# Gated linear attention and a squared-ReLU layer on one core: decays without a head mask, other fillers on TensorE, other due times

## The chip, the cores and the metric

The kernel runs on one core of a Trainium2 chip. The core has five engines with queues of their own: TensorE (PE in the profile, its weight loads PEld), VectorE (DVE), ScalarE (ACT), GpSimd (POOL) and SyncE (SP, which here only issues DMAs). The metric is device time of one execution in microseconds; the median of five runs of the kernel before is 180.68 us (179.46 to 181.27).

## The reference

For each of 4 batches and 8 heads a state of 48 x 48 is carried over 768 tokens; then all heads together, 384 wide, go through two dense layers.

```python
for t in range(S):
    state = alpha[:, :, t, :, None] * state + einsum('bhd,bhe->bhde', k[:, :, t], v[:, :, t])
    y[:, :, t] = einsum('bhd,bhde->bhe', q[:, :, t], state)
x = y.transpose(0, 2, 1, 3).reshape(3072, 384)
h = x @ w_in                 # 384 -> 2048
out = maximum(h, 0) ** 2 @ w_out   # 2048 -> 384
```

Inputs and the output are float32.

## The kernel before

**Units.** The tokens of a batch are cut into three stretches of 256, which makes 12 units, numbered so that units 0 to 3 are the first stretches of the four batches, 4 to 7 the second, 8 to 11 the last. A partition holds two neighbouring tokens (j = 0 and 1).

**Front of a unit** (`front`). The alphas become logarithms (ACT), and a matmul with a triangle of ones (`LINC`, `LSTR`) makes their running sums; ACT turns these into factors `EK` (by which k is multiplied) and `EQ` (for q). In the same step, called `m1`, products with the two columns of ones `ONES2` (L543, L604, L636) give each channel's sum over the whole unit, and ACT's exponential of it is `ACM`, the decay of the state from one unit to the next. Two heads share a weight load here, so such a product gives a column for each of the two heads; the mask matmul before it (`HSEL` by `HCOL`, L540, L601 and L634) puts -1000 where the row belongs to one head and the column to the other, so that the exponential is zero there. k and q with their factors (`QKS`) are transposed, on TensorE for units 0 to 2 and by a DMA on SyncE from unit 3 on (`tr0`, `tr1`, L711).

**Attention** (`scores`, `state`, `output`). Scores of k against q in psX and psZ (L889), masked on DVE into `PM` (L900); k by v for the state (L760), added up as `SMD`, `TMP` and `SBD`; the output from scores, v and state (L781 and L792, for units 0 to 2 L821 and L828). From unit 3 on the state products are cut by head, so that only the block of a head with itself is read. In units 0 to 2, `SMD` is multiplied by a mask `OWN`. The output is copied to bfloat16 (L920 or L922) and transposed into `XT`, on TensorE (L935) or by a DMA on SyncE (L941, units 4 to 10).

**Dense layers** (`moe`). Eight blocks of two times three matmuls of 256 columns (L992) into two PSUM banks; ReLU on ACT or DVE (L1000, L1002), square on DVE, ACT or POOL; then two output tiles of 16 matmuls of 384 columns (L1028) in four quarters each, copied (L1035) and stored from SyncE (L1038).

**What sets the order.** `Program.add` notes each operation with what it reads and writes, a cost and a due time. `Program.schedule` then goes through time with these costs: whenever an engine is free it takes, of the operations whose inputs are there, the one with the lowest due time. Operations with two possible engines go where they would end first. TensorE has one more rule: matmuls come in modes (whole array, row or column tiles), and if the one with the lowest due time has another mode, one in the present mode goes first when it is due not more than `AFFINITY` later:

```python
same = [x for x in avail[e] if x.mode[0] == mode and x.prio <= o.prio + self.AFFINITY]
```

The result is a fixed order on each engine; on the chip an engine runs its queue in that order and waits for semaphores. DMAs are part of the queue that issues them. Due times are 13000 apart from unit to unit, except for the first units, where `FRONT`, `ATTN` and `DENSE` (L357 to L359) give the start for a unit's front, attention and dense part. The last quarter of a unit's dense part, for example, is due at `DENSE` + 12787, its output at `ATTN` + 5600.

**Fillers.** `Program.fill` then goes along TensorE's order and puts matmuls of zeros (`ZERO`, into psO) in gaps, from the end of the clearing of `ZERO` on up to the first operation named `s2_` (the second dense product). It compares the planned start of the next operation with the time at hand.

**Loads.** SyncE issues the loads of units 0 and 1 at the start; GpSimd issues the v of unit 1, then w_in in two halves (as soon as unit 1's alpha has landed), unit 2's inputs and w_out in two halves.

Of the kernel before, what the change touches and what calls it, by code (L numbers as in the profile page):

```python
# [9 lines left out]
BF16 = mybir.dt.bfloat16  # L10
# [23 lines left out]
class Program:  # L34
# [177 lines left out]

    def fill(self, make, cost, until, gap, after, cold):


        new = []
        t = after.land + self.HOP
        cold += t
        for o in self.order["pe"]:
            while t < until and o.start - t > gap + (cost if t < cold else 0):  # L220
                f = Op({"pe": (make, cost)}, 0, "fill")
                f.idx = len(self.ops)
                f.eng, f.fn, f.cost = "pe", make, cost
                f.start, f.end = t, t + cost * (2 if t < cold else 1)
                f.deps = {after: True}
                self.ops.append(f)
                new.append(f)
                t = f.end
            new.append(o)
            t = max(t, o.end)  # L230
        for i, o in enumerate(new):
            o.pos = i
        self.order["pe"] = new
# [100 lines left out]
def bass_gla_recurrent__then__act_relu_squared_kernel(  # L334
# [10 lines left out]
    HD = H * D  # L345
# [10 lines left out]
    DMA_X = (4, 5, 6, 7, 8, 9, 10)  # L356
    FRONT = {0: 0, 1: 13357, 2: 25644, 3: 26390, 4: 37530, 5: 53567}  # L357
    ATTN = {1: 14618, 2: 26767, 3: 37301, 4: 52103}
    DENSE = {0: 19639, 1: 32250, 2: 48764, 3: 61983, 11: 158500}  # L359
    POOL_LOADS = {1: "v", 2: "akqv"}  # L360
# [39 lines left out]
    ONES2 = nc.alloc_sbuf_tensor("ones2", [128, 2], BF16)  # L400
    HSEL = nc.alloc_sbuf_tensor("hsel", [128, 128], BF16)
    HCOL = nc.alloc_sbuf_tensor("hcol", [128, H], BF16)
    OWN = nc.alloc_sbuf_tensor("own", [128, H], BF16)
# [21 lines left out]
    def fill(buf, val):  # L425
        return lambda e: e.memset(buf, val)  # L426
# [91 lines left out]
    def front_by_heads(g, p0):  # L518
# [7 lines left out]
        for x in range(2):  # L526
# [63 lines left out]
    def decays_by_token(g, p0, r, la):  # L590
# [5 lines left out]
        def m1(pe):  # L596
            pe.matmul(bank[:, 0, 0:HD], LINC[:], LAF[la][:, 0, :, 0:D], start=True, stop=False)
            pe.matmul(bank[:, 1, 0:HD], LINC[:], LAF[la][:, 0, :, 0:D], start=True, stop=False)
            pe.matmul(bank[:, 1, 0:HD], LINC[:], LAF[la][:, 1, :, 0:D], start=False, stop=True)
            pe.matmul(bank[:, 0, 0:HD], LSTR[:], LAF[la][:, 1, :, 0:D], start=False, stop=True)  # L600
            pe.matmul(bank[:, 0, HD:HD + H], HSEL[:], HCOL[:], start=True, stop=False, skip_group_check=True)  # L601
# [7 lines left out]
        add("pe", m1, pe_ns(4, HD) + pe_ns(9, 8), p0 + 300,  # L609
            reads=[("laf", la), ("linc",), ("lstr",), ("ones",), ("hsel",), ("hcol",)], writes=keys, name=f"m1{g}")  # L610
        add("act", lambda e: e.activation(EK[la][:], bank[:, 0:2, 0:HD], AF.Exp, scale=-1.0), act_ns(2 * HD), p0 + 500,
# [6 lines left out]
    def decays_by_pair(g, p0, r, la, last):  # L618
# [11 lines left out]
        def m1(incl):  # L630
            def run(pe):
                ins = pe.matmul(psW[:, 0:HD], (LINC if incl else LSTR)[:], LAB[la][:, :, 0:D])
                if incl and not last:
                    pe.matmul(psW[:, HD:HD + H], HSEL[:], HCOL[:], start=True, stop=False, skip_group_check=True)  # L634
                    for p in range(NPR):
                        ins = pe.matmul(psW[:, HD + 2 * p:HD + 2 * p + 2],  # L636
                                        LAB[la][:, 2 * p:2 * p + 2, :].rearrange("p h d -> p (h d)"), ONES2[:],
                                        start=False, stop=True, skip_group_check=True)
                return ins
            return run  # L640

        add("pe", m1(True), pe_ns(1, HD) + (0 if last else pe_ns(5, 8)), p0 + 300,
            reads=[("lab", la), ("linc",), ("ones",), ("hsel",), ("hcol",)], writes=[("ps", "W")], name=f"m1i{g}")
        add("act", lambda e: e.activation(EK[la][:, 1, :], psW[:, 0:HD], AF.Exp, scale=-1.0), act_ns(HD), p0 + 500,  # L644
# [413 lines left out]
    for st in ORDER:  # L1058
# [9 lines left out]
        else:  # L1068
            output(g, kind == "w")
            moe(g)  # L1070
    pr.schedule()
    pr.fill(lambda pe: pe.matmul(psO[:, 0:256], ZERO[:, 0:128], ZERO[:, 0:256], skip_group_check=True), 109,  # L1072
            min(o.start for o in pr.order["pe"] if o.name.startswith("s2_")), 250, zero, 4600)
    pr.place()
# [29 lines left out]
```

## Time and profile before

| | |
|---|---|
| median of five runs | 180.68 us (179.46 to 181.27) |
| the profiled execution | 179.96 us, of which the span of the trace is 178.1 us |
| PE | busy 170.2 us, 96%, 2287 matmuls |
| DVE | busy 120.9 us, 205 instructions |
| ACT | busy 119.8 us, 214 instructions |
| POOL | busy 15.9 us, 25 instructions |
| first dense block | starts at 19.09 us |
| fillers (L1072) | 72 of 256 columns, first at 1.25, last at 27.8 us |

How to read it: times in a trace count from the first instruction, so the execution is 1.9 us longer than the span. A line of a timeline has the start, the time to the end of the last of a group, the engine, the line of the kernel, the operation, what it writes and reads, and the count; matmuls overlap, so the distance between starts tells more than their durations. In a list of waits, the numbers are total time, how often, and the longest.

### The profile page before, as it was taken

What the parts mean: (1) busy time and instruction counts of PE and PEld (TensorE: products, weight loads), DVE (VectorE), ACT (ScalarE), POOL (GpSimd) and SP (SyncE); (2) the same over time, 40 slices, a digit from 0 to 9 for tenths busy, and PEclk for the clock granted to TensorE, in tenths of its full rate; (3) what the DMA queues carried; (4) which work ended last, traced back from release to release, by engine and by line L of the source; (5) the groups of instructions that cost most, each with busy time, mean ns of one, the idle gap of its engine ahead of it and who ended that gap; (6) DMA issues with size and microseconds to landing.
All of it is one profiled execution on the core that took longest, in us unless ns stands there. A gap on an engine that the chain in (4) does not pass through costs nothing.

```text
span 178.1 us, 5220 instructions
## 1 busy us (share of the span) xinstructions
PE 170.2 (96%) x2287; PEld 135.4 (76%) x2287; DVE 120.9 (68%) x205; ACT 119.8 (67%) x214; POOL 15.9 (9%) x25
## 2 busy tenths in 40 slices
PE   7899999998999899999999999998999999999994
PEld 5777788865778679778778777785778787698773
DVE  6478499888749789958689678589669646342130
ACT  5466498567888788679489379578578374475541
POOL 3160632020102002010000000000000000000000
PEclk9999999999999999999999999999999999999999
DMA  4999999999989896899898798799999690110112
GB/s 114 267 314 191 232 305 214 229 293 263 224 185 218 212 234 154 227 239 147 219 252 180 190 246 185 189 242 190 242 185 220 156 198 19 44 48 0 44 48 88
DMA packets 74616, 33.18 MB, mean 186 GB/s; under 512 B 69889, under 2 KB 73089, under 8 KB 74593
## 3 DMA queue, kind: packets, MB, share of 16 engines
q1 hardware_dynamic: 72944, 27.73, 69.5%
q0 software_dynamic: 1648, 5.11, 12.9%
q8 instruction: 18, 0.29, 0.6%
q14 instruction: 6, 0.04, 0.1%
HBM read 25.17 MB, written 4.72 MB: 168 GB/s over the span
## 4 chain that ended last, share of the span: by engine, by line
PE 61%; DMA 19%; ACT 8%; DVE 6%; SPq 4%; issue 2%; DVEq 0%
PE psWH L992 28%; PE psO L1028 21%; DMA raw<-in_v_dram 7%; DMA win<-in_moe_w_in_dram 4%; ACT rr L1000 3%; DMA raw<-in_alpha_dram 3%; SPq L514 3%; DMA raw<-in_q_dram 3%; DMA xt<-xbf 2%; DVE pm L900 2%; PE psX L792 2%; PE psZ L760 2%; PE psX L962 1%; PE psX L889 1%; PE psX L781 1%
## 5 line engine op out<-in xcount | busy, mean ns | idle before, releaser
L992 PE MATMUL psWH<-xt,win 128*128 128x256 bf16 x576 | 73.7, 275 | 1.4 <-DMA xt<-xbf 0.9
L992 PEld LDWEIGHTS psWH<-xt,win 128*128 128x128 bf16 x576 | 65.0, 145 | 6.6 <-DMA xt<-xbf 1.3
L1028 PE MATMUL psO<-wout,gt 128*128 128x384 bf16 x368 | 69.1, 327 | 0.1
L1000 ACT ACTIVATE rr<-psWH 128x512 bf16<-128x512 f32 x82 | 47.8, 594 | 22.0 <-PE psWH L992 20.6
L1028 PEld LDWEIGHTS psO<-wout,gt 128*128 128x128 bf16 x368 | 35.0, 98 | 18.2 <-ACT osb L1035 0.3
L1010 DVE TENSOR_TENSOR gt<-rr 128x1024 bf16<-128x1024 bf16 (+1 forms) x39 | 22.8, 586 | 21.9 <-ACT rr L1000 21.8
L1014 ACT ACTIVATE gt<-rr 128x1024 bf16<-128x1024 bf16 (+1 forms) x21 | 18.4, 875 | 0.6
L900 DVE TENSOR_TENSOR pm<-psX,caus 128x1024 bf16<-128x1024 f32 x12 | 14.6, 1217 | 3.8 <-PE psZ L889 3.8
L900 DVE TENSOR_TENSOR pm<-psZ,caus 128x1024 bf16<-128x1024 f32 x12 | 14.6, 1217 | 2.7 <-PE psZ L889 2.7
L695 DVE TENSOR_TENSOR qks<-raw,eq 128x384 bf16<-128x384 f32 x18 | 9.3, 553 | 8.1 <-DMA raw<-in_q_dram 8.1
L1035 ACT ACTIVATE osb<-psO 128x384 f32<-128x384 f32 x19 | 9.3, 491 | 6.3 <-PE psO L1028 5.8
L691 ACT ACTIVATE vbf<-raw 128x768 bf16<-128x768 f32 x8 | 6.7, 842 | 9.0 <-DMA raw<-in_v_dram 9.0
L1072 PE MATMUL psO<-zero 128*128 128x256 bf16 x72 | 11.0, 304 | 1.3 <-DVE zero L426 1.3
L920 ACT ACTIVATE xbf<-psX 128x768 bf16<-128x768 f32 x11 | 8.8, 803 | 4.0 <-PE psX L781 2.0
L700 DVE TENSOR_TENSOR qks<-raw,ek 128x768 bf16<-128x768 f32 x11 | 11.3, 1024 | 0.0
L1002 DVE TENSOR_SCALAR rr<-psWH 128x512 bf16<-128x512 f32 x14 | 9.6, 684 | 0.9 <-PE psWH L992 0.6
L1072 PEld LDWEIGHTS psO<-zero 128*128 128x128 bf16 x72 | 7.2, 108 | 2.8 <-DVE zero L426 1.2
L666 ACT ACTIVATE la<-raw 128x384 f32<-128x384 f32 x8 | 4.2, 520 | 3.4 <-DMA raw<-in_alpha_dram 3.4
L623 DVE TENSOR_TENSOR prd<-raw 128x384 f32<-128x384 f32 x8 | 4.5, 557 | 2.8 <-DMA raw<-in_alpha_dram 2.8
L653 DVE TENSOR_TENSOR ek<-ek,raw 128x384 f32<-128x384 f32 x10 | 5.5, 553 | 0.8 <-ACT ek L644 0.7
L626 ACT ACTIVATE lab<-prd 128x384 bf16<-128x384 f32 x10 | 5.2, 521 | 1.1 <-DVE prd L623 0.8
L644 ACT ACTIVATE ek<-psWH 128x384 f32<-128x384 f32 x10 | 4.9, 493 | 1.4 <-PE psWH L636 1.4
(121 smaller groups left out, 164.9 us busy)
## 6 DMA issues: line engine op xcount, KB each, us to landing
out_dram<-osb SPq DMA_DIRECT2D x23, 192.0 KB, 2.4
raw<-in_k_dram SPq DMA_DIRECT2D x11, 384.0 KB, 4.8
raw<-in_q_dram SPq DMA_DIRECT2D x11, 384.0 KB, 4.3
raw<-in_v_dram SPq DMA_DIRECT2D x10, 384.0 KB, 5.6
raw<-in_alpha_dram SPq DMA_DIRECT2D x10, 384.0 KB, 4.0
win<-in_moe_w_in_dram POOLq DMA_DIRECT2D x2, 768.0 KB, 9.4
wout<-in_moe_w_out_dram POOLq DMA_DIRECT2D x2, 768.0 KB, 9.3
raw<-in_v_dram POOLq DMA_DIRECT2D x2, 384.0 KB, 5.9
```

What stands on the lines that cost most here:

```text
L695: add("dve", lambda e, j=j, dst=dst: e.tensor_tensor(dst, RAW[r][:, 2, :, j, :].rearrange("p (n x) d -> p n x d", x=2), EQ[la][:, j].rearr ...
L700: add("dve", lambda e, a=a, E=E: e.tensor_tensor(QKS[qs][:, a, :, :, 0:D], RAW[r][:, 1 + a].rearrange("p h j d -> p j h d"), E[la][:].rear ...
L900: add("dve", lambda e, hf=hf, psT=psT: e.tensor_tensor(PM[pm][:, hf].rearrange("p r n j t -> p (r n) (j t)"), psT[:, :, :].rearrange("p r ...
L920: add("act", lambda e: e.activation(XBF[x2][:], psX[:, :, 0:HD], AF.Copy), act_ns(2 * HD), p0 + 6100, reads=[("ps", "X", 0), ("ps", "X", 1 ...
L992: ins = pe.matmul(psH[hb][:, i * T:(i + 1) * T], WIN[:, kk, hidden(fj)], mov, start=(kk == 0), stop=(kk == KT - 1))
L1000: add("act", lambda e, hb=hb, rr=rr: e.activation(rr, psH[hb], AF.Relu), act_ns(512), pu + 600, reads=[("ps", "H", hb)], writes=[("rr", rb ...
L1002: alts={"dve": (lambda e, hb=hb, rr=rr: e.tensor_scalar(rr, psH[hb], 0.0, None, ALU.max), dve_ns(512))})
L1010: add("dve", lambda e, dst=dst, sq=sq: e.tensor_tensor(dst, sq, sq, ALU.mult), 148 + k * 267, pu + 1200, reads=[("rr", rb, h) for h in ran ...
L1014: "act": (lambda e, dst=dst, sq=sq: e.activation(dst, sq, AF.Square), act_ns(k * 512))})
L1028: ins = pe.matmul(psS, GT[gt][:, fj, j, :], WOUT[:, fj, :], start=(fj == 0), stop=(fj == FT - 1))
L1035: add("act", lambda e, ob=ob, psS=psS: e.activation(OSB[ob][:], psS, AF.Copy), act_ns(DM), ps_ + 700, reads=[keyS], writes=[("osb", ob)], ...
L1072: pr.fill(lambda pe: pe.matmul(psO[:, 0:256], ZERO[:, 0:128], ZERO[:, 0:256], skip_group_check=True), 109, min(o.start for o in pr.order[" ...
```

## The change

The buffers `HSEL` and `HCOL`, the memsets that fill them and the mask matmul in each `m1` are left out; the first product with ones then starts its accumulation itself where the mask did. `ACM` therefore holds the channel's decay in the columns of both heads, and the state's blocks between two heads are no longer zeroed. The fillers end at the first operation named `s1_` (the first dense product) and come in two widths, 512 columns (cost 216, in gaps over 420) before 256 (cost 109, over 250). Most of the due times of units 1 to 5 are other numbers.

```diff
-    def fill(self, make, cost, until, gap, after, cold):
+    def fill(self, make, sizes, until, after, cold):
...
-            while t < until and o.start - t > gap + (cost if t < cold else 0):
-                f = Op({"pe": (make, cost)}, 0, "fill")
+            while t < until:
+                slow = 2 if t < cold else 1
+                fits = [(n, c) for n, c, gap in sizes if o.start - t > gap + (slow - 1) * c]
+                if not fits:
+                    break
+                n, c = fits[0]
+                f = Op({"pe": (make(n), c)}, 0, "fill")
...
-                f.start, f.end = t, t + cost * (2 if t < cold else 1)
+                f.start, f.end = t, t + c * slow
...
-    FRONT = {0: 0, 1: 13357, 2: 25644, 3: 26390, 4: 37530, 5: 53567}
-    ATTN = {1: 14618, 2: 26767, 3: 37301, 4: 52103}
-    DENSE = {0: 19639, 1: 32250, 2: 48764, 3: 61983, 11: 158500}
+    FRONT = {0: 0, 1: 11855, 2: 27782, 3: 24892, 4: 39487, 5: 52627}
+    ATTN = {1: 13665, 2: 25972, 3: 40856, 4: 50288}
+    DENSE = {0: 21894, 1: 33515, 2: 47958, 3: 58770, 11: 158500}
...
-    for buf, key in ((HSEL, "hsel"), (HCOL, "hcol"), (OWN, "own")):
-        add("dve", fill(buf[:], 0.0), 100, -2e6, writes=[(key,)])
-    for part, key, val in ((HSEL[0:1, 64:128], "hsel", -1000.0), (HSEL[32:33, 0:64], "hsel", -1000.0),
-                           (HCOL[0:1, 0:H:2], "hcol", 1.0), (HCOL[32:33, 1:H:2], "hcol", 1.0),
-                           (OWN[0:64, 0:H:2], "own", 1.0), (OWN[64:128, 1:H:2], "own", 1.0)):
-        add("dve", fill(part, val), 100, -2e6, reads=[(key,)], writes=[(key,)])
+    add("dve", fill(OWN[:], 0.0), 100, -2e6, writes=[("own",)])
+    for part in (OWN[0:64, 0:H:2], OWN[64:128, 1:H:2]):
+        add("dve", fill(part, 1.0), 100, -2e6, reads=[("own",)], writes=[("own",)])
...
-                pe.matmul(bank[:, HD:HD + 4], HSEL[:], HCOL[:, 0:4], start=False, stop=False, skip_group_check=True)
...
-            add("pe", m1, pe_ns(4, N) + pe_ns(5, 8), px + 300,
-                reads=[("laf", la, x), ("linc",), ("lstr",), ("ones",), ("hsel",), ("hcol",)], writes=key,
+            add("pe", m1, pe_ns(4, N) + pe_ns(4, 8), px + 300,
+                reads=[("laf", la, x), ("linc",), ("lstr",), ("ones",)], writes=key,
...
-                    pe.matmul(psW[:, HD:HD + H], HSEL[:], HCOL[:], start=True, stop=False, skip_group_check=True)
                     for p in range(NPR):
                         ins = pe.matmul(psW[:, HD + 2 * p:HD + 2 * p + 2],
                                         LAB[la][:, 2 * p:2 * p + 2, :].rearrange("p h d -> p (h d)"), ONES2[:],
-                                        start=False, stop=True, skip_group_check=True)
+                                        start=(p == 0), stop=True, skip_group_check=True)
...
-    pr.fill(lambda pe: pe.matmul(psO[:, 0:256], ZERO[:, 0:128], ZERO[:, 0:256], skip_group_check=True), 109,
-            min(o.start for o in pr.order["pe"] if o.name.startswith("s2_")), 250, zero, 4600)
+    pr.fill(lambda n: lambda pe: pe.matmul(psO[:, 0:n], ZERO[:, 0:128], ZERO[:, 0:n], skip_group_check=True),
+            ((512, 216, 420), (256, 109, 250)), min(o.start for o in pr.order["pe"] if o.name.startswith("s1_")), zero, 4600)
```

More of the change, by code (lines that the diff above doesn't have):

```diff
@@ L219, in fill @@
         for o in self.order["pe"]:
-            while t < until and o.start - t > gap + (cost if t < cold else 0):
-                f = Op({"pe": (make, cost)}, 0, "fill")
+            while t < until:
[5 more added lines that the diff above has]
+                f = Op({"pe": (make(n), c)}, 0, "fill")
                 f.idx = len(self.ops)
-                f.eng, f.fn, f.cost = "pe", make, cost
-                f.start, f.end = t, t + cost * (2 if t < cold else 1)
+                f.eng, f.fn, f.cost = "pe", make(n), c
+                f.start, f.end = t, t + c * slow
                 f.deps = {after: True}
@@ L400, in bass_gla_recurrent__then__act_relu_squared_kernel @@
     ONES2 = nc.alloc_sbuf_tensor("ones2", [128, 2], BF16)
-    HSEL = nc.alloc_sbuf_tensor("hsel", [128, 128], BF16)
-    HCOL = nc.alloc_sbuf_tensor("hcol", [128, H], BF16)
     OWN = nc.alloc_sbuf_tensor("own", [128, H], BF16)
@@ L600, in m1 @@
             pe.matmul(bank[:, 0, 0:HD], LSTR[:], LAF[la][:, 1, :, 0:D], start=False, stop=True)
-            pe.matmul(bank[:, 0, HD:HD + H], HSEL[:], HCOL[:], start=True, stop=False, skip_group_check=True)
             for p in range(NPR):
@@ L605, in m1 @@
                                     LAF[la][:, j, 2 * p:2 * p + 2, :].rearrange("p h d -> p (h d)"), ONES2[:],
-                                    start=False, stop=True, skip_group_check=True)
+                                    start=(p == 0 and j == 0), stop=True, skip_group_check=True)
             return ins
-        add("pe", m1, pe_ns(4, HD) + pe_ns(9, 8), p0 + 300,
-            reads=[("laf", la), ("linc",), ("lstr",), ("ones",), ("hsel",), ("hcol",)], writes=keys, name=f"m1{g}")
+        add("pe", m1, pe_ns(4, HD) + pe_ns(8, 8), p0 + 300,
+            reads=[("laf", la), ("linc",), ("lstr",), ("ones",)], writes=keys, name=f"m1{g}")
         add("act", lambda e: e.activation(EK[la][:], bank[:, 0:2, 0:HD], AF.Exp, scale=-1.0), act_ns(2 * HD), p0 + 500,
@@ L637, in run @@
                                         LAB[la][:, 2 * p:2 * p + 2, :].rearrange("p h d -> p (h d)"), ONES2[:],
-                                        start=False, stop=True, skip_group_check=True)
+                                        start=(p == 0), stop=True, skip_group_check=True)
                 return ins
             return run
-        add("pe", m1(True), pe_ns(1, HD) + (0 if last else pe_ns(5, 8)), p0 + 300,
-            reads=[("lab", la), ("linc",), ("ones",), ("hsel",), ("hcol",)], writes=[("ps", "W")], name=f"m1i{g}")
+        add("pe", m1(True), pe_ns(1, HD) + (0 if last else pe_ns(4, 8)), p0 + 300,
+            reads=[("lab", la), ("linc",), ("ones",)], writes=[("ps", "W")], name=f"m1i{g}")
         add("act", lambda e: e.activation(EK[la][:, 1, :], psW[:, 0:HD], AF.Exp, scale=-1.0), act_ns(HD), p0 + 500,
```

## The prediction

> **What bounds the kernel now.** I read the page's first two parts, then the waits of TensorE, the chain that ended last, and the timelines of TensorE and SyncE around each edit.
>
> The page, share of each engine and the granted clock:
>
> ```profile
> PE 170.2 (96%) x2287; PEld 135.4 (76%) x2287; DVE 120.9 (68%) x205; ACT 119.8 (67%) x214; POOL 15.9 (9%) x25
> ...
> PEclk9999999999999999999999999999999999999999
> ```
>
> TensorE is busy 96% at a clock that never falls in any slice. The chain of waits of the first 21 us says what the start is:
>
> ```profile
> 3.03 2.54 SPq L514
> 5.57 0.04 issue
> 5.61 5.17 DMA raw<-in_alpha_dram
> 10.78 0.30 issue
> 11.08 7.87 DMA win<-in_moe_w_in_dram
> 18.95 0.14 issue
> 19.09 1.50 PE psWH L992 x12
> ```
>
> So the first dense block starts at 19.09 because the first half of w_in lands at 18.95; no TensorE work is on that path. From 19.09 to the last product TensorE is the path. All its idle time above the view's threshold, in the waits of TensorE after 18 us:
>
> ```profile
> PE psWH L992 <- DMA xt<-xbf: 0.9, 1, 0.9
> PE psX L821 <- DVE qks L700: 0.7, 1, 0.7
> PE psX L889 <- DVE la L668: 0.6, 1, 0.6
> PE psWH L992 <- DMA win<-in_moe_w_in_dram: 0.4, 1, 0.4
> ```
>
> 2.6 us in four places (124.8, 42.5, 60.0 and 19.1). Whatever is to move the time by over 1%, 1.8 us, must move the w_in landing, remove most of these, or make new waits.
>
> **The masks.** Nine mask matmuls go: two in unit 0 (L540), one in unit 1 (L601), one each in units 2 to 7 (L634). The weight load beside L634, in the timeline of unit 2:
>
> ```profile
> 27.25 0.33 PE L632 MATMUL psWH<-lab,linc 128*128 128x384 bf16 x1
> 27.25 0.10 PEld L634 LDWEIGHTS psWH<-hcol,hsel 128*128 128x128 bf16 x1
> 27.41 0.17 PE L634 MATMUL psWH<-hcol,hsel 128*128 128x8 bf16 x1
> 27.41 0.17 PEld L636 LDWEIGHTS psWH<-ones,lab 128*128 128x128 bf16 x4
> 27.44 0.24 PE L636 MATMUL psWH<-ones,lab 128*128 128x2 bf16 x4
> 27.54 0.60 PE L1072 MATMUL psO<-zero 128*128 128x256 bf16 x4
> ```
>
> The durations overlap, so starts are what counts: L632 holds the array from 27.25 to 27.41 with the mask there or not, the mask from 27.41 to 27.44, the four sums to 27.54. The mask's own load (27.25, 0.10) lies inside L632's time. One mask costs 0.03 us, six cost 0.18. The page's group for the chain agrees: L634 is 0.01 on it. Units 0 and 1 lie before 19.09: L540 takes 0.07 each (5.07 to 5.14, 5.84 to 5.91), L601 0.02. That is hidden: after the first of these, DVE waits for k ("DVE qks L567 <- DMA raw<-in_k_dram: 2.8" in the waits), and behind it stands w_in. If that cover went, it would be 0.16 more.
>
> [...]
>
> **The memsets.** Two whole buffers and four parts, six short memsets, go from DVE (2.07 to 2.58 us). DVE's next use that somebody waits for is at 6.97, when k has landed. Worth nothing; it would be 0.5 us if k came at once.
>
> **The fillers.** The page has 72 of 256 columns:
>
> ```profile
> L1072 PE MATMUL psO<-zero 128*128 128x256 bf16 x72 | 11.0, 304 | 1.3 <-DVE zero L426 1.3
> ```
>
> The timeline has 65 of them before 19.09, in gaps of 15, 6, 16, 2, 19, 1 and 6, then three at 23.00 and four at 27.54. After the change each gap before the first dense block is packed with 512-wide ones while more than 420 ns is left (636 while the clock is taken as cold), then with 256-wide ones while more than 250 is left (359 cold). Each old gap is its count times 109 ns (218 in the first, cold) and the rest that was too short for one more, so the new counts are about 7+1, 2+2, 7+2, 0+2, 9+2, 0+1 and 2+2: 27 wide and 12 narrow. A wide one is not in the trace; start to start a narrow one took 0.110 us warm and 0.213 cold, so a wide one takes at least one narrow, 0.110, and at most two, 0.22 and 0.43. I take two, since columns are what is streamed. In both versions a warm gap stays open for 0.14 to 0.25 us at its end, so the fillers end within 0.11 us of where they ended. The delay that they give to the matmul behind them (the mask product was done at 14.71, the fillers hold TensorE until 15.26) stays, and it is covered by the w_in landing: xt of unit 0 is ready at 18.15, 0.8 us early. The late ones fill real waits: at 23.00 until the ReLU ends at 23.29, at 27.54 until the copy of xt ends at 28.08 and the dense block starts at 28.14. Without them TensorE is idle 0.34 and 0.60 us there and starts its block at the same time, or up to 0.05 sooner. Together 0, bounds -0.1 and +0.1. What could go wrong is the clock. The row nearest is the wait of 0.9 us before 124.8 with a granted clock of 1.00 in that window and the next; the new holes are shorter.
>
> **The due times.** FRONT, ATTN and DENSE are priorities: at each step the planner gives the engine the ready operation with the lowest number. So they matter only where two operations are ready at once and their order flips. I went through the trace's order with the new numbers. For units 0 to 2 most numbers move by 1 to 2 us but the pairs that meet do not cross: unit 1's output goes from 20218 to 19265 and the dense quarter ready beside it from 24514 to 26769, so both orders put the output first; unit 2's front from 25644 to 27782 still meets only unit 1's dense block (32250, then 33515). Two flips remain, both from DENSE[3], 61983 to 58770:
> - ReLU and square of unit 3's last blocks (67458 becomes 64245) pass the last exponentials of unit 6's decay (65520) on ACT, near 70 us. TensorE has 1.3 us of second products queued there (71.22) and unit 6's q only lands at 74.19. Worth 0.
> - The last quarter of unit 3's second product (74770 becomes 71557) against unit 5's output (70600). TensorE is in another tile mode, and a same-mode operation within AFFINITY, 2500, goes first: the limit is 73100, so the quarter now goes ahead. Today the output runs at 77.90 and the quarter at 78.95. The quarter costs the same in either place; the output ends 0.65 later, its copy on ACT (79.39) near 80.04. The store of unit 3 is ready sooner and comes ahead of unit 5's xt transposition on SyncE:
>
> ```profile
> 77.19 3.93 SPq L711 DMA_TRANSPOSE kqt<-qks  x2
> 81.16 2.26 SPq L941 DMA_TRANSPOSE xt<-xbf  x1
> 83.47 0.58 SPq L1038 DMA_DIRECT2D out_dram<-osb  x1
> ```
>
> SyncE is held by unit 6's two transpositions until 81.12, so the later copy costs nothing, but the store's 0.58 now stands before xt. Its landing, 81.16 + 3.8 (DMA issues of that window) = 84.96, becomes about 85.6; unit 5's dense block starts at 85.83. That leaves 0.2 us. Bounds: the store's issue took 0.33 to 1.33 elsewhere, and with that and the longest landing of an xt (2.4 after its issue, against 1.55) it lands at 87.2, 1.3 us late. Below zero too: up to the 0.9 and 0.6 of waits in units 3 to 8 could go if the shift lines up. I take 0, from the 0.58 of the nearest row.
>
> **The sum.** Masks -0.18, memsets 0, fillers 0, due times 0: the profiled execution's 179.96 becomes 179.8. It was 0.7 below the median 180.68 of the five runs; carried over, **180.5 us**.
>
> **The rivals.**
> 1. *Faster: another order.* I followed the order by hand; one more flip near 40 to 62 us could remove the waits at 42.5 and 60.0 (0.7 + 0.6), with the masks 1.5 us: 179.2; with the 0.9 at 124.8 too, 178.3. For it: five due times moved by 2 to 3.5 us. Against it: both waits end on the decay chain (DVE L700 and L668), whose pairs I found uncrossed. 0.16.
> 2. *Slower: the store before xt.* Place: SyncE at 81.2. Price: what xt lands beyond 85.83, 0 to 1.3 us, so 180.5 to 181.8; it decides from a delay of 0.87 us on, and a slowdown of over 1% needs 2.7, a second entry in front as well. For it: SyncE's issues there took up to 2.26 us, and at 121.14 an xt issued behind two stores is the one whose landing TensorE waits 0.9 for. Against it: at 108.01 and 133.99 xt stands behind two stores too, and no wait for it is listed. 0.21.
> 3. *The fillers do not cover.* The clock falls as it stands for the first fillers, 0.213 us each against 0.110 and 3.2 us long, once around 28; half of 3.2 lost is 1.6: 182.1. Nothing in the row of clocks speaks for it. 0.03.
>
> Forecast: 0.60. **Chances.** 1% of 180.7 is 1.8 us, about what a measurement of this kernel can tell (the five runs spread over 1.8). Faster by more: half of rival 1, and 0.06 of the forecast, whose runs stray and whose order I may have missed: 0.14. Slower by more: rival 3, a quarter of rival 2 and 0.06 of the forecast: 0.14. Within 1%: 0.72. **Range**: down to rival 1's 179.2 less 0.4 for the straying of a median, 178.8; up to rival 2's 181.8 and 0.2 of the same, 182.0.
>
> **What the profile after would show.** 2287 - 9 - 33 = 2245 matmuls on TensorE and about 199 instructions on DVE; about 39 fillers, the wide ones near 0.22 apart; the first dense block at 19.1 within 0.2; TensorE idle at 23.0 and 27.5; PEclk all 9. The sums at L636's place start 0.16 after the matmul before them. The quarter of unit 3 stands ahead of unit 5's output near 77.9, and a store ahead of xt on SyncE near 81. The prediction is wrong if the order on TensorE before 68 us differs, if xt of unit 5 lands after its turn, or if a clock digit falls.

## The result and the profile after

The changed kernel is **slower by 0.72%**: median 180.70 us (178.45 to 184.09, 51 runs) against 179.96 us (176.93 to 185.74, 91 runs) for the kernel before, ratio 1.0072, 95% interval 1.0051 to 1.0093. The means of all runs are 180.81 and 180.02, a difference of +0.79 ± 0.46 us (0.44%). The ratio of a comparison leaves out runs more than 1.5% above the fastest of their kernel; as the runs here scatter by more than that without any sign of a disturbance, and the fastest of 35 runs tends to lie lower than the fastest of 12, the experiments below are given as differences of means over all runs of a batch (kernels run together on one chip), with 1.96 standard errors, and with the ratio where the two say different things.

The profiled execution of the changed kernel took 179.41 us (span 177.7), less than that of the kernel before (179.96, 178.1). One profile of each therefore doesn't show the slowdown; that needs many runs and, for its place, many profiles. Lines of the changed kernel are three lower than before (L989 for L992, L633 for L636).

The page after, engine shares and clock:

```profile
PE 168.9 (95%) x2243; PEld 131.2 (74%) x2245; DVE 120.3 (68%) x196; ACT 121.4 (68%) x215; POOL 19.2 (11%) x27
...
PEclk9999999999999999999999999999999999999999
```

2245 weight loads, as forecast, and no drop of the clock. DVE has 196 instructions where 199 were forecast, POOL 27 and ACT 215: operations went to other engines, a first sign of another order. (These are net counts. By the orders written out for the experiments below, 17 operations change their engine, 12 of them of units 0 to 2.) The chain of waits of the start:

```profile
4.75 5.59 DMA raw<-in_alpha_dram
10.34 0.30 issue
10.64 8.23 DMA win<-in_moe_w_in_dram
18.86 0.14 issue
19.00 0.85 PE psWH L989 x6
19.85 0.35 PE psX L886 x16
```

The first dense block still starts when w_in has landed, at 19.00. But it is cut after six matmuls by unit 1's scores (L886); before, twelve ran first and the scores came at 20.52. The waits of TensorE after 18 us:

```profile
PE psX L778 <- DVE pm L897: 1.0, 1, 1.0
PE psWH L989 <- DMA win<-in_moe_w_in_dram: 0.7, 1, 0.7
PE psX L818 <- DVE qks L697: 0.4, 1, 0.4
```

The waits of 0.9 (xt) and 0.6 (L889) are absent here, and a new one of 1.0 us has come: unit 4's output (L778), at 64.7 us, waits for the masked scores.

The place of a mask, the whole timeline near 27 us:

```profile
27.18 0.33 PE L630 MATMUL psWH<-lab,linc 128*128 128x384 bf16 x1
27.18 0.31 PEld L633 LDWEIGHTS psWH<-ones,lab 128*128 128x128 bf16 x4
27.34 0.24 PE L633 MATMUL psWH<-ones,lab 128*128 128x2 bf16 x4
```

The sums start 0.16 after the product, in the mask's old place, as forecast. The fillers' group and SyncE near 81 us:

```profile
L1069 PE MATMUL psO<-zero 128*128 128x512 bf16 (+1 forms) x37 | 9.3, 393 | 1.5 <-DVE zero L429 1.3 <-issue 0.2
```

```profile
76.73 4.91 SPq L708 DMA_TRANSPOSE kqt<-qks  x2
81.69 0.58 SPq L1035 DMA_DIRECT2D out_dram<-osb  x1
82.31 1.25 SPq L938 DMA_TRANSPOSE xt<-xbf  x1
```

39 fillers are in the program (39 weight loads; two matmul records are missing). The store stands ahead of xt on SyncE, and xt landed at 85.04 in time for its block: no wait for an xt is in the list.

### The profile page after: what moved, and what is told of

It is laid out like the page before. It is cut to its first block, busy times and chain, and to the rows that moved or that the text cites. A ratio compares the mean times of both kernels' runs of the same rounds, so it can differ in the third digit from the quotient of the medians.

```text
span 177.7 us, 5127 instructions
## 1 busy us (share of the span) xinstructions
PE 168.9 (95%) x2243; PEld 131.2 (74%) x2245; DVE 120.3 (68%) x196; ACT 121.4 (68%) x215; POOL 19.2 (11%) x27
## 4 chain that ended last, share of the span: by engine, by line
PE 64%; DMA 16%; SPq 7%; ACT 7%; DVE 5%; issue 1%; DVEq 0%
PE psWH L989 27%; PE psO L1025 25%; DMA raw<-in_q_dram 6%; DMA raw<-in_alpha_dram 5%; DMA win<-in_moe_w_in_dram 5%; DVE pm L897 3%; SPq L708 3%; SPq L514 2%; ACT rr L997 2%; PE psX L789 2%; PE psX L886 2%; PE psX L959 1%; PE psX L778 1%; PE psZ L757 1%; ACT eq L643 1%
## 5 line engine op out<-in xcount | busy, mean ns | idle before, releaser
L989 PE MATMUL psWH<-xt,win 128*128 128x256 bf16 x576 | 74.2, 275 | 1.0 <-DMA win<-in_moe_w_in_dram 0.7
L989 PEld LDWEIGHTS psWH<-xt,win 128*128 128x128 bf16 x576 | 64.9, 145 | 5.9 <-ACT rr L997 1.0
L1011 ACT ACTIVATE gt<-rr 128x1024 bf16<-128x1024 bf16 (+1 forms) x23 | 19.6, 852 | 1.0 <-DVE rr L999 0.4
L897 DVE TENSOR_TENSOR pm<-psX,caus 128x1024 bf16<-128x1024 f32 x12 | 14.6, 1217 | 4.1 <-PE psZ L886 4.1
L897 DVE TENSOR_TENSOR pm<-psZ,caus 128x1024 bf16<-128x1024 f32 x12 | 14.6, 1217 | 2.0 <-PE psZ L886 2.0
L692 DVE TENSOR_TENSOR qks<-raw,eq 128x384 bf16<-128x384 f32 x18 | 9.9, 588 | 6.8 <-DMA raw<-in_q_dram 6.6
L917 ACT ACTIVATE xbf<-psX 128x768 bf16<-128x768 f32 x10 | 8.1, 806 | 5.6 <-PE psX L778 4.1
L999 DVE TENSOR_SCALAR rr<-psWH 128x512 bf16<-128x512 f32 x15 | 10.3, 684 | 1.1 <-PE psWH L989 0.7
L1069 PE MATMUL psO<-zero 128*128 128x512 bf16 (+1 forms) x37 | 9.3, 393 | 1.5 <-DVE zero L429 1.3
L697 DVE TENSOR_TENSOR qks<-raw,ek 128x768 bf16<-128x768 f32 x11 | 10.4, 947 | 0.0
L1069 PEld LDWEIGHTS psO<-zero 128*128 128x128 bf16 x39 | 3.8, 106 | 5.4 <-issue 1.7
L852 DVE TENSOR_TENSOR smd<-psZ,sbd 128x384 bf16<-128x384 f32 x8 | 4.4, 555 | 2.7 <-PE psX L778 2.7
L621 DVE TENSOR_TENSOR prd<-raw 128x384 f32<-128x384 f32 x7 | 3.9, 556 | 2.7 <-DMA raw<-in_alpha_dram 2.6
```

Source lines behind the costliest of these rows:

```text
L692: add("dve", lambda e, j=j, dst=dst: e.tensor_tensor(dst, RAW[r][:, 2, :, j, :].rearrange("p (n x) d -> p n x d", x=2), EQ[la][:, j].rearr ...
L697: add("dve", lambda e, a=a, E=E: e.tensor_tensor(QKS[qs][:, a, :, :, 0:D], RAW[r][:, 1 + a].rearrange("p h j d -> p j h d"), E[la][:].rear ...
L897: add("dve", lambda e, hf=hf, psT=psT: e.tensor_tensor(PM[pm][:, hf].rearrange("p r n j t -> p (r n) (j t)"), psT[:, :, :].rearrange("p r ...
L917: add("act", lambda e: e.activation(XBF[x2][:], psX[:, :, 0:HD], AF.Copy), act_ns(2 * HD), p0 + 6100, reads=[("ps", "X", 0), ("ps", "X", 1 ...
L989: ins = pe.matmul(psH[hb][:, i * T:(i + 1) * T], WIN[:, kk, hidden(fj)], mov, start=(kk == 0), stop=(kk == KT - 1))
L999: alts={"dve": (lambda e, hb=hb, rr=rr: e.tensor_scalar(rr, psH[hb], 0.0, None, ALU.max), dve_ns(512))})
```

## The experiments

**How the parts were taken apart.** The change has three parts: masks (M), order (O, from the due times and new costs) and fillers. Since the planner reorders on small differences of cost, single parts were built with the order of one of the two kernels written out as a table:

```diff
+    PIN = {"pe": ("... p0_1 s1_0_1 ...").split(), "dve": ..., "act": ..., "pool": ..., "sp": ...}
...
-                    o = min(avail[e], key=lambda o: (o.prio, o.idx))
+                    ready = [o for o in avail[e] if not o.name or o.name == due[e]]
+                    o = min(ready, key=lambda o: (o.prio, o.idx))
```

**One part alone.** `e1_masks`: the masks out, order and fillers of the kernel before.

> The masks, their buffers and memsets are left out, and nothing else: the order on every engine is written out and is that of the kernel before, the fillers are the old ones. By the prediction's own step, six masks of 0.03 us each on TensorE's path: ratio to before 0.999 (0.998 to 1.000). If the masks' weight loads were not hidden: 0.996. If the slowdown of 0.7% came from this part (sums of both heads in the state, another start of the accumulation): 1.007.

`e2_order`: masks and fillers of before, the order of the changed kernel.

> Masks and the 256-wide fillers up to the first second product stay; the order on every engine is written out and is that of the changed kernel (unit 1's attention ahead of unit 0's dense blocks from 19 us on, other engines for a dozen operations between 24 and 36 us, unit 5's output behind unit 3's last quarter, a store ahead of an xt on SyncE). Theory A, the order costs the time: 1.007 to 1.009. Theory B, the fillers cost it: 1.000. Theory C, the masks: 1.000.

`e3_fill`: only the new `fill` with its two widths, ending at the first dense block.

> Only the fillers are the new ones: 512 columns where they fit, none after the first dense block. Masks, order and due times are those of before. Theory A (order): 1.000. Theory B (fillers: the holes of 0.34 and 0.60 us at 23.0 and 27.5, or the wide ones ahead of the first block, lower the clock or hold up a matmul): 1.007, and then a clock under 1.000 or a later first dense block than 19.1.

`e4_after`: the changed kernel once more, beside these.

> The changed kernel again, beside the three parts on the same chip: 1.005 to 1.009, and the three ratios less one should add up to it within 0.003 if the parts do not act on each other.

Measured against the kernel before in the same batch: masks -0.21 ± 0.66, order -0.06 ± 0.96, fillers +0.49 ± 0.80 (ratio 1.0087, interval 1.0028 to 1.0146), the whole +0.87 ± 0.81. The whole is slower again, and of the parts only the fillers point the same way. The three sum to +0.22, short of the whole by 0.65, which is within their scatter; by the ratios they sum to +0.0160 where the whole has +0.0082, further apart than the 0.003 expected.

**Each part left out.** `e5_masks_order` is the changed kernel with the old fillers, `e6_masks_fill` with the old order, `e7_order_fill` with the masks back.

> The changed kernel with the old fillers (256 columns, up to the first second product); masks out and order as changed. After the first runs the fillers alone stood 0.6 us above before, the order alone about level, the masks alone 0.2 below. Theory B (fillers cost the time): 0.998 to 1.001. Theory A (order): 1.006 to 1.009. Theory D (no part alone, only masks and order together, or the scatter of DMA landings): 1.004 or more with e6 level.

> The changed kernel with the order of before on every engine; masks out, new fillers. Theory B (fillers): 1.003 to 1.006. Theory A (order): 0.998 to 1.000.

> The changed kernel with the masks, their buffers and memsets back in; order and fillers as changed. Both theories: as the changed kernel or 0.001 above it, 1.006 to 1.010. If this one is level with before, the masks' removal is what costs.

Measured: +0.14 ± 0.81, 0.00 ± 0.72, +0.45 ± 0.85 (one run of 244.94 us left out of the last, see the end). Each is too close to zero to name a part by itself. The old fillers bring the kernel level (ratio 0.9997, 0.9950 to 1.0044), as the fillers' theory had it, but so, within their intervals, do the old order (1.0033) and the masks put back (1.0028, where both theories had 1.006 to 1.010).

**The width and the end of the fillers.** `e8_wide_late` is the kernel before with two widths, the fillers still running up to the first second product; `e9_wide_late_again` repeats it in another batch. `e10_narrow_short` is the kernel before with its narrow fillers ending at the first dense block, `e11_no_fill` has none, and `e12_null` leaves out one of the 15 of the first gap.

```diff
-            min(o.start for o in pr.order["pe"] if o.name.startswith("s2_")), 250, zero, 4600)
+            min(o.start for o in pr.order["pe"] if o.name.startswith("s1_")), 250, zero, 4600)
```

> The kernel before with 512-wide fillers where they fit, but up to the first second product as it was (two at the place of each late gap). Theory B1 (the end of the fillers costs: holes at 23.0 and 27.5): 1.000. Theory B2 (the wide ones ahead of the first block cost): 1.004 to 1.009. Theory A (order): 1.000.

> The same program as e8_wide_late (before, wide fillers, same gaps filled for the same time), once more. If wide fillers cost time: 1.006 to 1.010 again. If e8's 1.6 us were scatter of DMA landings: 0.997 to 1.003.

> The kernel before with its 256-wide fillers ending at the first dense block: the seven at 23.0 and 27.5 us are left out. If the holes there cost: 1.003 to 1.006. If only the width costs, or nothing: 0.998 to 1.002.

> The kernel before without any filler. If the fillers' part in the clock is what matters, TensorE starts its dense block at the low clock of the first fillers (0.213 us for 256 columns instead of 0.110) for some 3 us: 1.6 us or 1.009 slower, and a clock digit under 9 at 19 us. If they do nothing there: 1.000.

> The kernel before with 14 fillers of 256 columns instead of 15 ahead of the first matmul of unit 0; nothing waits for them, and the first dense block waits for w_in. By every theory of a cost in the code: 1.000 within 0.002. If a change that costs nothing moves the time by 0.004 or more, the 0.7% are of that kind: where the DMA landings fall.

Measured: +1.62 ± 0.65 and +0.82 ± 0.96 for wide and late; -0.67 ± 0.85 for narrow and short; +1.34 ± 1.25 for none (6 runs); -0.41 ± 0.84 for one less. Wide fillers cost (e9's mean alone leaves it open; its ratio is 1.0088, 1.0044 to 1.0132), and so does having none. Ending narrow ones early may gain by the mean, but not by the ratio (1.0029, 0.9986 to 1.0073).

The loss of e11 isn't the one that was expected for it. Its first dense block begins at 19.09 as before, and behind the second its matmuls start 0.11 us apart, as before, though the matmuls ahead of the block had run at half pace (0.32 us from start to start for 384 columns at 12 us, against 0.16 at 27 us before). In the second product, of which the table below tells, it is level at 40 us (39.82) and late at 66 (66.89), as with wide fillers.

**Undoing the width alone.** `e13_after_narrow`:

```diff
-            ((512, 216, 420), (256, 109, 250)), min(o.start for o in pr.order["pe"] if o.name.startswith("s1_")), zero, 4600)
+            ((256, 109, 250),), min(o.start for o in pr.order["pe"] if o.name.startswith("s1_")), zero, 4600)
```

> The changed kernel with its fillers 256 columns wide again (65 of them: 15, 6, 15, 2, 20, 1, 6), still ending at the first dense block; masks out and due times as changed. Theory W, the width of the fillers costs about 1.2 us and nothing else in the change costs anything: level with the kernel before or up to 0.7 under it, and no wait of TensorE at unit 4's output near 64.5. Theory O, the order costs it (the width only went along with it in the runs so far): 0.2 to 0.9 us over the kernel before. Between -0.2 and +0.2 it speaks for W with ending the fillers early worth nothing.

-1.07 ± 0.77 against the kernel before, and no wait at unit 4's output. By the means, the changed kernel with narrow fillers isn't slower, and theory O falls in this run. By the ratio it is level (1.0031, 0.9985 to 1.0076), and e18, below, doesn't repeat the gain: that the order costs a little isn't excluded.

**Width or number of instructions.** `e14_pairs` splits each wide filler:

```diff
+            if n == 512:
+                pe.matmul(psO[:, 0:448], ZERO[:, 0:128], ZERO[:, 0:448], skip_group_check=True)
+                n2 = 2
+            else:
+                n2 = n
+            return pe.matmul(psO[:, 0:n2], ZERO[:, 0:128], ZERO[:, 0:n2], skip_group_check=True)
```

> The changed kernel, each 512-column filler split into one of 448 columns and one of 2 behind it, so that the first 19 us hold about as many instructions on TensorE (66) as with narrow fillers (65), in the same time. Theory N, what matters is the number of instructions that TensorE has gone through by then (where its instructions are loaded beside the data): back to the time of the kernel before or up to 0.7 under it. Theory W, wide matmuls themselves: 0.5 to 1.0 us over the kernel before, with the wait near 64.5 in the profile.

-0.45 ± 1.10: inside what theory N gave, and 0.95 under the lower end of what theory W gave, which is 1.7 standard errors. The wait at unit 4's output is there (1.5 us), as W had it. It leans to N and settles nothing.

**In which gaps.** `e15_wide_first` has wide ones in the first gap alone, `e16_wide_rest` (with `slow == 1`) in all others. The edit, against the new `fill`:

```diff
-                fits = [(n, c) for n, c, gap in sizes if o.start - t > gap + (slow - 1) * c]
+                fits = [(n, c) for n, c, gap in sizes if o.start - t > gap + (slow - 1) * c and (n == 256 or slow == 2)]
```

> The kernel before with wide fillers in the first gap alone (8 in place of 15), the rest narrow as before. If the width costs in the first gap, where the clock is cold: +0.8 to +1.6 us over the kernel before. If it costs in the later gaps: within 0.3 of it. If it is the number of instructions, 7 fewer of 30: about a quarter of the effect, +0.2 to +0.4, not to be told from nothing.

> The kernel before with narrow fillers in the first gap and wide ones in the later gaps (4, 9, 2, 10, 1, 4, 2, 2 in place of 6, 16, 2, 19, 1, 6, 3, 4). If the width costs in the first gap: within 0.3 of the kernel before. If in the later gaps, or by the number of instructions (23 of 30 fewer): +0.6 to +1.6 us.

-0.45 ± 1.06 and +0.19 ± 0.86 (ratio 1.0092, interval 1.0043 to 1.0142). Wide fillers in the first gap (0.42 us apart there in after's trace, 0.22 in the later gaps) cost nothing that can be seen (ratio 1.0036, 0.9983 to 1.0088); the later ones do by the ratio, but their mean isn't told from nothing and lies under the +0.6 to +1.6 expected.

**All runs together.** A fit gives each part of the change one number, chosen so that their sums come closest to all measured means (least squares). Over the means of the result and of all these kernels but `e11_no_fill`, with an offset for each batch and a run's scatter of 1.35 us (single kernels have 0.7 to 1.8), it gives: masks out -0.04 ± 0.45, order +0.27 ± 0.45, **wide fillers +1.06 ± 0.38** (split: first gap +0.21 ± 0.57, later gaps +0.85 ± 0.57), **ending early -0.57 ± 0.47**, and e14's fillers, with a term of their own, +0.24 ± 0.91. The four terms of the change sum to +0.72, against +0.79 measured: +0.49 ± 0.42 from the two of the fillers and +0.23 ± 0.45 from masks and order. What is left over is no more than scatter (a chi-square of 14.0 with 13 degrees of freedom; e17 and e18, below, count as their kernels without the exchange). By the ratios the eight kernels with wide fillers (e3, e4, e6 to e9, e16, e17) stand at 1.0028 to 1.0123, mean 1.0076, and the eight with narrow ones (e1, e2, e5, e10, e12, e13, e15, e18) at 0.9997 to 1.0046, mean 1.0025. The width holds either way; the gain of ending early doesn't show in the ratios.

**Where the loss lies.** Nine profiles have narrow fillers behind the first gap (before, e1, e2, e5, e10, e12, e13, e15, e18), eight wide ones (after, e3, e4, e6, e8, e9, e16, e17; e7's profile ran at another clock). The mean time at which certain matmuls of the second product (L1028) start, from the traces, with one standard error:

```
matmul of the second product      0       23       46       69       92      184      final
narrow, us                     32.56    40.09    46.57    57.67    65.71   101.73   172.03
wide, us                       32.49    39.97    46.79    58.04    66.36   102.53   172.61
wide later by                  -0.07    -0.12    +0.22    +0.38    +0.64    +0.80    +0.58
standard error                  0.29     0.26     0.40     0.38     0.36     0.33     0.50
the same without e3            -0.01    -0.03    -0.10    +0.08    +0.40    +0.58    +0.38
```

Nothing is lost up to 40 us, when the last filler has been done for about 12 us. The loss comes between 40 and 66 and is still there at 102. A good part of it is e3's one long wait (2.5 us at 43.6); without that profile it comes between 58 and 66, and it is less sure (+0.40 with a standard error of 0.28 at 66). From 110 on, waits for xt transpositions, which come in 15 of 19 profiles (these, e11 and e14; 0.5 to 2.2 us, near 112 or 125), cover it.

What TensorE waits for in that stretch is unit 4's output, at about 64.5: by the lists of waits for 0.2 to 1.0 us in five of the eight wide profiles (after, e4, e6, e8, e9; not in e16, not in e17, of which below, and not in e3, where TensorE was 2.5 us late already), for 1.5 in e14, and in none of the narrow ones. (In e11 the output waits 0.8, but for unit 5's v on ACT.) VectorE after, in the timeline:

```profile
59.64 0.95 DVE L697 TENSOR_TENSOR qks<-raw,ek 128x768 bf16<-128x768 f32 x1
62.36 1.02 DVE L692 TENSOR_TENSOR qks<-raw,eq 128x384 bf16<-128x384 f32 x2 [1.77 <-DMA raw<-in_q_dram]
63.30 1.22 DVE L897 TENSOR_TENSOR pm<-psX,caus 128x1024 bf16<-128x1024 f32 x1
64.44 1.21 DVE L897 TENSOR_TENSOR pm<-psZ,caus 128x1024 bf16<-128x1024 f32 x1
```

The masked scores of unit 4 (L897) stand behind unit 5's q (L692), and that waits 1.77 us for its load. `e17_swap` and `e18_narrow_swap` exchange the two, with wide and with narrow fillers:

```diff
-             ... lb5 ekm5 eqm0_5 eqm1_5 mk0_4 mk1_4 sd4 ...
+             ... lb5 ekm5 mk0_4 mk1_4 eqm0_5 eqm1_5 sd4 ...
```

> The changed kernel with one pair of pairs exchanged in VectorE's order near 61 us: the two causal-mask products of unit 4 (L897) go ahead of the two scalings of q of unit 5 (L692), everything else as in the changed kernel, wide fillers included. Theory D: the wide fillers cost their time through q of unit 5 landing late, which holds the masks of unit 4 behind it on VectorE and so unit 4's output on TensorE at 64.5; then that wait is gone and the kernel is level with the one before or up to 0.6 under it. If the wait is only a sign of the loss and not its path: the wait is gone and the kernel is still 0.5 to 1.0 us over the one before, with as much idle time elsewhere. Third way: unit 5's transpositions then start up to 1 us later and the loss moves to unit 5's scores.

> The same exchange in the changed kernel with 256-column fillers (the kernel that was 1.1 us under the one before). With narrow fillers there was no wait at unit 4's output to remove, so theory D expects the exchange to do nothing here: 0.6 to 1.3 us under the kernel before. If the exchange by itself helps or hurts by the later transpositions of unit 5, that shows here: outside that interval.

VectorE in e17:

```profile
59.38 0.95 DVE L777 TENSOR_TENSOR qks<-raw,ek 128x768 bf16<-128x768 f32 x1
60.24 1.22 DVE L977 TENSOR_TENSOR pm<-psX,caus 128x1024 bf16<-128x1024 f32 x1
61.38 1.22 DVE L977 TENSOR_TENSOR pm<-psZ,caus 128x1024 bf16<-128x1024 f32 x1
62.51 1.02 DVE L772 TENSOR_TENSOR qks<-raw,eq 128x384 bf16<-128x384 f32 x2
```

The idle time and the wait on TensorE are gone, and e17 is still +1.04 ± 0.68 over the kernel before. **Theory D falls** by this time: the wait goes along with the loss, it is not its only path. (e17's one profile is not late at 66 us, 65.39 where the table above has 65.71 for narrow ones, so where e17 loses is not seen.) e18 was +0.41 ± 0.70, above the interval that it was given; with e13 that makes -0.33 ± 0.52 for the changed kernel with narrow fillers. Between e17 and e18, which differ in the width alone, lie 0.63 ± 0.76: this pair by itself doesn't tell the width from nothing.

**What shifts by 40 us.** While the work on TensorE keeps level up to 40 us, one thing does not: the packets of the queue that the page calls instruction. The page's DMA queues, of before and of after:

```profile
q8 instruction: 18, 0.29, 0.6%
```

```profile
q8 instruction: 17, 0.28, 0.6%
```

The 18 packets are of 16384 bytes each in the DMA records. From the start of one to the start of the next, TensorE starts 248 matmuls and weight loads on the mean in before (180 to 336) and 250 in after (156 to 329). That the queue carries TensorE's instructions is an inference from this and from the table that follows, in which the third packet comes later the fewer matmuls the fillers have; no run shows it directly. From the DMA records of the traces, the start of q8's third and fourth packet, the fourth's duration, and the time that SyncE took to issue unit 4's four loads at about 40 us:

```
                              third    fourth   took      four issues together
narrow, 9 profiles          27.3-29.5  37.2-39.1  0.88-1.94  3.25-4.27, mean 3.74
wide, 8 profiles            30.0-31.6  38.4-40.5  0.88-1.58  3.33-4.98, mean 4.23
e14, pairs                    28.1      37.9      0.88       3.60
e11, none                     34.4      44.1       -         4.75
```

SyncE in that stretch, first of e13 (narrow), then of after (wide):

```profile
39.31 0.36 SPq L1035 DMA_DIRECT2D out_dram<-osb  x1
39.71 0.43 SPq L514 DMA_DIRECT2D raw<-in_alpha_dram  x1
40.19 0.70 SPq L514 DMA_DIRECT2D raw<-in_k_dram  x1
40.94 1.21 SPq L514 DMA_DIRECT2D raw<-in_q_dram  x1
42.19 1.13 SPq L514 DMA_DIRECT2D raw<-in_v_dram  x1
```

```profile
38.66 0.36 SPq L1035 DMA_DIRECT2D out_dram<-osb  x1
39.16 0.51 SPq L514 DMA_DIRECT2D raw<-in_alpha_dram  x1
39.71 0.67 SPq L514 DMA_DIRECT2D raw<-in_k_dram  x1
40.42 2.75 SPq L514 DMA_DIRECT2D raw<-in_q_dram  x1
43.22 1.05 SPq L514 DMA_DIRECT2D raw<-in_v_dram  x1
```

With wide fillers the fourth packet falls at about 40 us, amid the issues of unit 4's loads (after: at 40.4, taking 1.58 us), with narrow ones mostly ahead of them (e13: at 38.2, 0.88 us). The issue of q, 0.69 to 1.34 us in the nine narrow profiles, takes 1.74 to 2.75 in six of the eight wide ones. That fits e14, whose packets fall as with narrow fillers. But it is not shown to be the cause: e11 has a long issue of q (2.69) with no q8 packet near it, and e9 a short one (0.69) though slow in the mean.

These are the loads of unit 4; the q of unit 5, for which VectorE waits in after, is issued eleven entries later in SyncE's queue. The delay goes on to there. SyncE in after and in e13:

```profile
57.39 0.44 SPq L514 DMA_DIRECT2D raw<-in_q_dram  x1
```

```profile
56.62 0.44 SPq L514 DMA_DIRECT2D raw<-in_q_dram  x1
```

The mean start of some of SyncE's issues, over the same profiles as above:

```
                     unit 4's q   unit 4's v   unit 4's transposition   unit 5's q
narrow, us              40.51        41.66             50.61               56.35
wide, us                40.38        42.29             51.54               57.23
wide later by           -0.13        +0.63             +0.93               +0.87
standard error           0.27         0.31              0.29                0.26
```

SyncE is late from the long issue of unit 4's q on, before TensorE is. e14 doesn't fit in here: its issue of unit 4's q is short (1.30), and yet its issue of unit 5's q is as late as with wide fillers (57.31). **Shown is that the width costs, and the profiles put the loss behind 40 us, on SyncE first; through what stays open.** No run moved the packets, or SyncE's issues, and left all else in place.

## Why the prediction was wrong

- **The fillers, "together 0, bounds -0.1 and +0.1": the step that failed.** The fit puts this term at +0.49 ± 0.42: the width costs 1.06 ± 0.38, ten times the upper bound, and the early end gives back 0.57 ± 0.47. With masks and order at +0.23 ± 0.45 together, it is the larger part of the slowdown, as far as the scatter lets one say. The step priced what fillers do on TensorE up to the next dense block, and there it was right: wide ones ran 0.22 us apart (seven from 7.66 to 8.96), the first block began at 19.00, its matmuls 0.11 apart, the clock at 9. It took that for the whole. Fillers are instructions too: about the same columns in 26 fewer instructions ahead of the first block were followed by a loss after 40 us, whose path stays open.
- **"From 19.09 to the last product TensorE is the path."** True of the chain, too narrow to go by. The page's DMA row of before stood mostly at 8 or 9 tenths, and never under 6, from 4 to 147 us, and the longest of the four waits, the 0.9 at 124.8, ended on a landing. Such waits come and go from profile to profile (after has none for an xt, e1 one of 2.2), and a wait that comes or goes weighs more than any of the terms that were summed. The prediction never used that row:

```profile
DMA  4999999999989896899898798799999690110112
```

- **"The pairs that meet do not cross": wrong.** It followed due times at dense quarters and outputs and missed the rule of the tile mode at the first block: unit 1's scores (`ATTN` + 3800) were due at 18418 and are at 17465, the second group of six dense matmuls (`DENSE` + 812) at 20451 and now at 22706, which is more than `AFFINITY`, 2500, behind. So the scores go after six matmuls instead of twelve, and 12 operations of units 0 to 2 change their engine. A different order on TensorE before 68 us was one of the prediction's own signs of being wrong. Another order was rival 1's mechanism, with 0.16. Its forecast of a gain did not come: the order is worth +0.27 ± 0.45, not told from nothing. The idle times at 23.0 and 27.5 were forecast for the old order; after, there is 0.20 at 23.35 and none is marked near 27.5.
- **Masks, -0.18: not contradicted.** The trace shows the sums 0.16 behind the product; the times give -0.04 ± 0.45, too wide to tell 0.18 from 0. The first load for the sums has its record at 27.18 to 27.28, inside the time of L630's matmul (27.18, 0.33), both on 128 rows.
- **Memsets, 0**: nothing waits for VectorE at their place after either.
- **The two late flips: right.** The last quarter of unit 3 went ahead of unit 5's output (which starts at 78.98 after, at 77.90 before), the store ahead of xt, and xt was in time. Rival 2 did not decide.
- **Rival 3, the clock at the fillers**: it did not come. PEclk is all 9 in after. That row alone would not do, since it stands at 9 over the slow fillers of the first 4 us too (256 columns 0.213 us apart in before, 512 columns 0.42 in after), but the dense matmuls at 19 us start 0.11 apart, as before.
- **The chances.** "1% is about what a measurement can tell" went by five runs; 142 runs gave an interval of 0.2% to each side, and 0.7% is told from nothing.

By the fit, the changed kernel with narrow fillers is about 1 us faster than the change as made; whether it beats the kernel before is not settled (-1.07 ± 0.77 and, with the exchange, +0.41 ± 0.70).

## What to carry to other kernels

Where the page shows the DMA engines near full (mostly 8 or 9 tenths here), look also at what an edit may do to the order in which transfers meet, the packets of the instruction queue among them: 26 fewer dummy matmuls in a covered stretch, before 19 us, were followed by a loss between 40 and 66. Take the effect of a part from many runs, in several batches, with the part undone alone; a single profile of each here had the sign wrong. A wait that appears with the slowdown is a suspect, and an edit that removes just that wait tests whether it is the path.

## What the runs showed of the hardware

**The granted clock was 0.50 behind a wait of 2.5 us.** In e3's profile TensorE waited once for long, for v of unit 3. The waits between 36 and 60 us, and then the windows around it (stretch, its length, busy time of PE, PEld, DVE, ACT and POOL with counts, granted clock, DMA share, GB/s):

```profile
PE psX L826 <- ACT vbf L696: 2.5, 1, 2.5
```

```profile
42.00:44.00 2.00, 0.42 (x8) 0.37 (x8) 0.15 (x1) 1.41 (x3) 0.00 (x0) 0.86 0.95 244
44.00:46.00 2.00, 2.00 (x53) 1.53 (x51) 1.43 (x3) 0.65 (x2) 0.00 (x0) 0.50 0.99 236
46.00:48.00 2.00, 2.00 (x15) 1.27 (x14) 0.05 (x1) 1.55 (x4) 0.00 (x0) 0.79 1.25 269
```

The clock is 0.50 in the 2 us from 44, 0.79 in the next 2 and, in the window behind these, from 48 on, 1.00. By these windows the wait cost its 2.5 us and then, as an estimate, about 1.4 us more (half of 2 us, then 0.21 of 2 us). In e1 and e14, whose longest waits after 18 us were of 2.2 us, the mean granted clock of the profiled execution was 1.00, in e3 0.99. It is one case: that the wait brought the fall on, and that it would do so again, is not shown.

**One execution ran at two thirds of the clock.** It is e7's profiled one, 244.94 us at a mean granted clock of 0.662; the page has

```profile
span 243.2 us, 5149 instructions
...
PEclk9666666666666666666666666666666666666666
```

with the clock down from the second slice on. It happened in one of 507 runs (the granted clock of all others was 0.98 or more), and nothing in the kernel is known to bring it on.

**The scatter.** The kernel before had standard deviations of 1.0 to 1.8 us within a batch and means of 178.2 to 180.2 us from batch to batch, two of them on the same chip (179.9 and 178.2). That is over the effect looked for, so only kernels of one batch were set against each other.
